# Attention steps with values, denominators and scores of different units side by side, MLP pieces ahead of each attention part, and a second output bank

## The chip, the cores and the metric

The kernel runs on one core of a Trainium2 chip. The metric is device time in microseconds (us). Medians are quoted with the range of the runs. The engines are called PE (TensorE matmul), PEld (its weight loads), ACT (ScalarE), DVE (VectorE), POOL (GpSimd) and SP (SyncE, which issues transfers).

## The reference, cut to what matters

```python
# attention: 8 batches, 8 heads, 576 positions, head size 64
scores = q @ k.T / 8
mask = |i - j| <= 32, or i or j is one of 8 global positions
attn = softmax(where(mask, scores, -1e9))
x = (attn @ v), heads side by side            # 4608 tokens x 512
# MLP
h = x @ w_in                                  # 512 -> 2048
g = h + sin(alpha * h)**2 / (alpha + 1e-9)
out = g @ w_out                               # 2048 -> 512
```

## The kernel before

A batch's attention is 8 units (4 pairs of heads, 2 halves of the sequence). A unit has three stages on PE:

- `stage_Q`: 12 score matmuls into `Sp` (two banks of PSUM, the memory that PE writes its results to), then Exp on ACT into `E` and a multiplication by the mask on DVE.
- `stage_D`: two matmuls with ones into `den` (one bank). ACT takes Ln and Exp of it, which gives the reciprocal `rec`; DVE sums the global columns into `gd`.
- `stage_V`: 12 value matmuls into `num` (one bank). DVE multiplies it by `rec` into `xT`, and sums its global columns into `gn`.

`stage_T` transposes keys and queries of one pair of heads on PE. DVE copies the keys out of the bank `Kps` to `kTw` (0.85 us).

The MLP is done in nine chunks of 512 tokens. `mm1(c)` is the first projection: 16 slots of four matmuls into one of six banks `hb`; then Sin on ACT (`Sb`), a square (`S`) on POOL, DVE or ACT, and an addition on DVE into `H2b`, which frees the bank. `mm2(c)` is the output projection: four token tiles of four pieces of four matmuls. It fills the attention of the next batch, so batch p's attention is mixed with `mm2(p-1)`, and `mm1(p)` follows. The last stage mixes `mm1(8)` with `mm2(7)`, and `mm2(8)` ends the program. The program gives every engine its instructions in the order written. `psA`, `psB` and `psC` in the code are pools of banks.

```python
    def attention(b, psA, t_at):
        ...
        def first(j):
            if j == -2:
                nc.scalar.preload_act_table_set("natural_log_exp_and_others")
            if j + 2 < NUN:
                Es[j + 2] = stage_Q(psA, b, *units[j + 2])
            if 0 <= j + 1 < NUN:
                recs[j + 1] = stage_D(psA, *units[j + 1], Es[j + 1], gd)
            if j + 1 == NUN:
                stage_Gd(gd, gr)
        def second(j):
            if j >= 0:
                stage_V(psA, b, *units[j], Es.pop(j), recs.pop(j), gn)
        parts = []
        for j in range(-2, NUN):
            parts += [partial(first, j), partial(second, j)]
        ...
    # mm2: the tile is copied out by ACT, then stored
                        nc.scalar.copy(out=osb[:], in_=ops[:])
    # which engine squares slot nt of mm1
    sq_late = lambda nt: nc.vector if nt % 5 == 4 else nc.gpsimd
    # batch p > 0: banks of the four tiles, and pieces after each part
                    fill = mm2(p - 1, H2[p - 1], ((psC, "ops"),) * 3 + (((psA, "den") if p > 1 else (psC, "ops")),))
                    counts = [2, 0, 1, 0] + [1, 0] * (NUN)
    # what is left of fill runs after the last part
```

The softmax here doesn't subtract the row's maximum and nothing guards it: scores larger than these inputs give would overflow.

Of the kernel before, what the change touches and what calls it, by code (L numbers as in the profile page):

```python
# [18 lines left out]
def kernel(  # L19
# [11 lines left out]
    nc = tc.nc  # L31
    P = 128
    BF = DT.bfloat16
# [24 lines left out]

    const = ctx.enter_context(tc.tile_pool(name="const", bufs=1))
    qkp = ctx.enter_context(tc.tile_pool(name="qkp", bufs=2))  # L60
    epool = ctx.enter_context(tc.tile_pool(name="epool", bufs=4))
    rpool = ctx.enter_context(tc.tile_pool(name="rpool", bufs=3))
    gpool = ctx.enter_context(tc.tile_pool(name="gpool", bufs=2))

# [266 lines left out]
    def stage_Q(psA, b, hp, hf):  # L331
        Sp = psA.tile([P, 2, CH], F32, name="Sp")
        for u in range(NU):
            i = hf * NU + u
            for t, pr in heads:
                nc.tensor.matmul(  # L336
                    out=Sp[:, t, u * QC : (u + 1) * QC],
                    lhsT=kTw[hp][pr, i, :], rhs=qT[hp][pr, i, :],
                    start=True, stop=True, skip_group_check=True,
                )  # L340
        E = epool.tile([P, 2, EW], BF, name="E")
        nc.scalar.activation(out=E[:], in_=Sp[:, :, 0:EW], func=AF.Exp, scale=scale)  # L342
        mk = MASK[:, hf * NU : (hf + 1) * NU, :].rearrange("p u c -> p (u c)")
        nc.vector.tensor_tensor(  # L344
            out=E[:], in0=E[:], in1=mk[:, None, :].to_broadcast([P, 2, EW]), op=ALU.mult
        )
        return E
# [44 lines left out]
    def stage_Gd(gd, gr):  # L392
        nc.vector.tensor_tensor(out=gr[:], in0=gd[:, 0], in1=gd[:, 1], op=ALU.add)
        nc.vector.reciprocal(out=gr[:], in_=gr[:])
# [11 lines left out]

    units = [(hp, hf) for hp in range(NHP) for hf in range(2)]
    NUN = len(units)

    def attention(b, psA, t_at):  # L410

        Es, recs = {}, {}
        gn = gpool.tile([P, 2, NHP, NG], F32, name="gn")
        gd = gpool.tile([P, 2, NHP, NG], F32, name="gd")
        gr = gpool.tile([P, NHP, NG], F32, name="gr")

        def first(j):
            if j == -2:
                nc.scalar.preload_act_table_set("natural_log_exp_and_others")
            if j + 2 < NUN:  # L420
                Es[j + 2] = stage_Q(psA, b, *units[j + 2])
            if 0 <= j + 1 < NUN:
                recs[j + 1] = stage_D(psA, *units[j + 1], Es[j + 1], gd)
            if j + 1 == NUN:
                stage_Gd(gd, gr)

        def second(j):
            if j >= 0:
                stage_V(psA, b, *units[j], Es.pop(j), recs.pop(j), gn)

        parts = []
        for j in range(-2, NUN):
            parts += [partial(first, j), partial(second, j)]
        for hp, i in t_at.items():
            parts[i] = partial(chain, parts[i], partial(stage_T, b, hp, psA, "qp"))
        return parts, partial(stage_G, b, gn, gr)

    def chain(*fs):
        for f in fs:
            f()  # L440
# [42 lines left out]
    def mm2(c, H2b, pools):  # L483
        slots = []
        st = {}
        G4 = 4
        for ts in range(CH // P):
            for g in range(NT // G4):
                def slot(ts=ts, g=g):
                    if g == 0:  # L490
                        pool, tag = pools[ts]
                        st["o"] = pool.tile([P, DM], F32, name=tag)
                    ops = st["o"]
                    for nt in range(g * G4, (g + 1) * G4):
                        nc.tensor.matmul(  # L495
                            out=ops[:], lhsT=H2b[:, nt, ts * P : (ts + 1) * P],
                            rhs=w_out[:, nt, :],
                            start=(nt == 0), stop=(nt == NT - 1),
                        )
                    if g == NT // G4 - 1:  # L500
                        osb = osbp.tile([P, DM], F32, name="osb")
                        nc.scalar.copy(out=osb[:], in_=ops[:])  # L502
                        r0 = c * CH + ts * P
                        nc.sync.dma_start(out=out[r0 : r0 + P, :], in_=osb[:])
                slots.append(slot)
        return slots
# [12 lines left out]
    def with_extra(parts, extra, start, per):  # L519
        for i in range(start, len(parts)):  # L520
            k_ = (i - start) * per
            if extra[k_ : k_ + per]:
                parts[i] = partial(chain, parts[i], *extra[k_ : k_ + per])
        return extra[(len(parts) - start) * per :] if len(parts) > start else extra
# [19 lines left out]
        for i in range(4)  # L544
    ]

    sq_late = lambda nt: nc.vector if nt % 5 == 4 else nc.gpsimd
    sq_early = lambda nt: nc.vector if nt % 2 else nc.scalar

    ctx.enter_context(tc.manual_schedule())  # L550
    H2 = {}
    NP_ = 2 * (NUN + 2)
    for p in range(NCH):
        fill = []
        late = []
        if p < B:
            with phase_pool("psA", 1) as psA:
                if p == 0:
                    stage_T(0, 0, psA, "qp")
                    globals_all()  # L560
                    for hp in range(NHP):
                        globals_in(0, hp, nc.vector)
                    stage_T(0, 1, psA, "qp")
                    globals_v_all()
                    shift_v(0)
                    global_v(0)
                    parts, last = attention(0, psA, {2: 7, 3: 11})
                    with_extra(parts, w_loads, 6, 1)
                    parts[6] = partial(chain, parts[6], pool_regs)
                    late = load_slots(1, True)  # L570
                    counts = [0] * NP_
                else:
                    fill = mm2(p - 1, H2[p - 1], ((psC, "ops"),) * 3 + (((psA, "den") if p > 1 else (psC, "ops")),))
                    parts, last = attention(p, psA, {2: 4, 3: 8})
                    counts = [2, 0, 1, 0] + [1, 0] * (NUN)
                    if p == 1:
                        shift_v(1)
                        global_v(1)
                        for hp in range(NHP):
                            globals_in(1, hp, nc.vector)  # L580
                        pre = [fill.pop(0) for _ in range(6)]
                        chain(*pre[:4])
                        stage_T(1, 0, psA, "qp")
                        chain(*pre[4:])
                        stage_T(1, 1, psA, "qp")
                    if p + 1 < B:
                        ld = load_slots(p + 1, p == 1)
                        if p == 1:
                            late = ld[5:]
                            ld = ld[:5]  # L590
                            with_extra(parts, ld, 12, 1)
                        else:
                            with_extra(parts, ld, 0, 2)
                        for hp in range(NHP):
                            i_ = (10, 12, 14, 16)[hp]
                            parts[i_] = partial(chain, parts[i_], partial(globals_in, p + 1, hp))
                run(parts + [last], counts + [0], fill)
        else:
            fill = mm2(p - 1, H2[p - 1], ((psC, "ops"),) * 4)
        if p == 0:  # L600
            setup.release()
            hpool = ctx.enter_context(tc.tile_pool(name="hpool", bufs=2))
            spool = ctx.enter_context(tc.tile_pool(name="spool", bufs=4))
            osbp = ctx.enter_context(tc.tile_pool(name="osbp", bufs=2))
        with phase_pool("psB", 6) as psB:
            H2[p] = hpool.tile([P, NT, CH], BF, name="H2b")
            m1 = mm1(p, H2[p], psB, sq_early if p < 2 else sq_late)
            if late:
                with_extra(m1, late, 0, 2)
            if 1 <= p and p + 1 < B:  # L610
                i_ = (10, 13)
                m1[i_[0]] = partial(chain, m1[i_[0]], partial(shift_v, p + 1), partial(global_v, p + 1), partial(stage_T, p + 1, 0, psB, "hb"))
                m1[i_[1]] = partial(chain, m1[i_[1]], partial(stage_T, p + 1, 1, psB, "hb"))
            run(m1, [1] * NT if p == B else [0] * NT, fill if p == B else [])
            if p == NCH - 1:
                for s in mm2(p, H2[p], ((psC, "ops"), (psB, "hb")) * 2):
                    s()
# [30 lines left out]
```

## Time and profile before

| | before |
|---|---|
| median of 4 runs (range) | 404.38 us (401.99 to 405.27) |
| profiled execution, span | 400.5 us |
| PE / ACT / POOL / DVE busy | 85 / 64 / 63 / 59% |
| one period in the middle (batch and its first projection) | 40.4 us |
| of it: PE idle before the first scores | 1.84 us |

The first lines of the page give span and busy time of each engine (share of the span, number of instructions).

```profile
span 400.5 us, 8548 instructions
...
PE 341.6 (85%) x3157; PEld 169.6 (42%) x3208; DVE 236.1 (59%) x549; ACT 256.4 (64%) x437; POOL 250.9 (63%) x394
```

A busy share of 85% does not say where PE is held, so the timeline is read next. Its columns are start and length in us, engine, source line, operation, output and inputs, and in brackets the idle time of the engine before it and what ended that. This is a steady attention step on PE, without transposes:

```profile
203.34 0.37 PE L375 MATMUL num<-E,VW 128*64 128x56 bf16 x12
203.65 0.33 PE L336 MATMUL Sp<-qT,kTw 64*128 64x56 bf16 x12
203.91 0.33 PE L352 MATMUL den<-E,ones 128*64 128x336 bf16 x2
204.17 1.04 PE L495 MATMUL ops<-w_out,H2b 128*128 128x512 bf16 x4
205.14 0.38 PE L375 MATMUL num<-E,VW 128*64 128x56 bf16 x12
```

Starts are to be compared, as ends of matmuls are modelled: 0.31, 0.26, 0.26 and 0.97 us, in all 1.80 us. The shape `128*64` or `64*128` is the part of the array that an instruction uses; it changes four times a step.

At the end of a first-projection stage PE does nothing while DVE makes additions, because the first scores are to be written into banks that these additions free:

```profile
230.25 1.89 PE L458 MATMUL hb<-xT,w_in 128*128 128x512 bf16 x8
233.98 0.33 PE L336 MATMUL Sp<-qT,kTw 64*128 64x56 bf16 x12 [1.84 <-DVE H2b L448]
234.24 1.68 PE L495 MATMUL ops<-w_out,H2b 128*128 128x512 bf16 x7
...
232.53 2.71 DVE L448 SCALAR_TENSOR_TENSOR H2b<-S,recipT,hb 128x512 bf16<-128x512 bf16 x4
```

Over the program the view of waits has for PE (total us, times, longest):

```profile
PE Sp L336 <- DVE H2b L448: 11.5, 6, 2.3
...
PE hb L458 <- POOL xT L402: 6.6, 2, 3.3
```

The second line is the end of batches 0 and 1, where no piece is left to cover POOL's copies of the global tokens. In batch 1 the first matmuls after that wait of 3.31 us run at half clock (the granted clock is 0.50 from 90.7 to 97.5 us), so 43 matmuls take 12.30 us:

```profile
92.15 12.30 PE L458 MATMUL hb<-xT,w_in 128*128 128x512 bf16 x43 [3.31 <-POOL xT L402]
```

The shorter idle (five times 1.84 to 1.85 us, once 2.28) is followed by half clock too, in one of its six occurrences in this execution: 0.50 from 275.0 to 278.5 us. The windows view (stretch, its length, busy time of PE, PEld, DVE, ACT, POOL, granted clock, DMA share, GB/s) around 274 us shows it:

```profile
272.00:274.00 2.00, 0.45 (x3) 0.09 (x1) 2.00 (x4) 1.81 (x3) 0.98 (x2) 1.00 0.00 0
274.00:276.00 2.00, 1.71 (x17) 0.83 (x17) 1.97 (x4) 1.26 (x2) 2.00 (x4) 0.76 0.05 3
276.00:278.00 2.00, 2.00 (x17) 0.61 (x14) 0.00 (x0) 0.00 (x0) 2.00 (x3) 0.50 1.54 98
```

In the last stage ACT copies the last tile of chunk 7, and the next tile, in the same bank, waits 0.67 us for it:

```profile
382.26 0.59 ACT L502 COPY osb<-ops 128x512 f32<-128x512 f32 x1
...
382.89 3.61 PE L495 MATMUL ops<-w_out,H2b 128*128 128x512 bf16 x16 [0.67 <-ACT osb L502]
```

### The profile page before, as it was taken

Reading aid. Unit: us, or ns where it says so; the run is one execution under the profiler, and the core shown is the slowest. Engines: PE = TensorE matmul, PEld = TensorE weight load, DVE = VectorE, ACT = ScalarE, POOL = GpSimd, SP = SyncE. Lnnn points to the kernel's source line nnn. Section 1 sums busy time; section 2 is a strip of 40 time slices with the busy share of each in tenths; the row PEclk is TensorE's granted clock in tenths of the full one; section 3 lists DMA queues with packets and bytes.
Section 4 is the critical chain, followed back from the end, with each engine's and each line's share of the span. In section 5 each row is a group of like instructions: output and inputs, shape, how many; then the busy total and the mean of one; then the engine's idle time right before and its main releaser. Section 6 shows DMA issues by size and latency. Waiting matters only on the chain.

```text
span 400.5 us, 8548 instructions
## 1 busy us (share of the span) xinstructions
PE 341.6 (85%) x3157; PEld 169.6 (42%) x3208; DVE 236.1 (59%) x549; ACT 256.4 (64%) x437; POOL 250.9 (63%) x394
## 2 busy tenths in 40 slices
PE   1137599877979997999899989998999899989996
PEld 0126244443435443444454445443544354434442
DVE  7826388571976297619762877286736873673330
ACT  1057495884988578748784878486838783855421
POOL 8934493329794398929892988398928401874410
PEclk9999999996999999999999999998999999999999
DMA  6999999349999319931993289627924001001012
GB/s 54 146 144 178 202 148 139 46 73 73 160 119 115 107 21 68 172 95 35 59 165 100 46 54 147 114 55 50 153 68 97 1 28 55 26 2 49 32 52 79
DMA packets 133723, 35.31 MB, mean 88 GB/s; under 512 B 123314, under 2 KB 128178, under 8 KB 133682
## 3 DMA queue, kind: packets, MB, share of 16 engines
q0 software_dynamic: 122560, 19.02, 66.4%
q1 hardware_dynamic: 8034, 15.54, 13.4%
q10 hardware_dynamic: 3088, 0.21, 0.8%
q8 instruction: 25, 0.41, 0.4%
q14 instruction: 16, 0.13, 0.1%
HBM read 38.42 MB, written 9.44 MB: 119 GB/s over the span
## 4 chain that ended last, share of the span: by engine, by line
PE 50%; POOL 14%; ACT 12%; issue 11%; DVE 11%; POOLq 1%; ACTq 0%
PE ops L495 23%; PE hb L458 8%; ACT Sb L465 7%; DVE H2b L448 7%; POOL S L473 7%; PE den L495 5%; PE num L375 4%; PE Sp L336 3%; PE den L352 3%; DVE kTw L310 2%; ACT S L471 2%; PE hb L495 2%; POOL KS L95 2%; POOL QS L95 1%; POOL VW L107 1%
## 5 line engine op out<-in xcount | busy, mean ns | idle before, releaser
L458 PE MATMUL hb<-xT,w_in 128*128 128x512 bf16 x559 | 134.9, 387 | 10.1 <-POOL xT L402 6.6
L448 DVE SCALAR_TENSOR_TENSOR H2b<-S,recipT,hb 128x512 bf16<-128x512 bf16 x144 | 101.2, 742 | 53.5 <-POOL S L473 53.5
L473 POOL TENSOR_TENSOR S<-Sb 128x512 bf16<-128x512 bf16 x91 | 94.2, 1063 | 43.5 <-ACT Sb L465 38.6
L465 ACT ACTIVATE Sb<-hb,alphaT 128x512 bf16<-128x512 f32 x144 | 95.1, 686 | 40.6 <-PE hb L458 36.1
L495 PE MATMUL ops<-w_out,H2b 128*128 128x512 bf16 x414 | 109.3, 383 | 4.1 <-issue 1.3
L458 PEld LDWEIGHTS <-w_in 128*128 128x128 bf16 x576 | 56.8, 99 | 79.8 <-issue 19.0
L495 PEld LDWEIGHTS <-H2b 128*128 128x128 bf16 x576 | 51.4, 98 | 60.3 <-issue 8.9
L342 ACT ACTIVATE E<-Sp 128x672 bf16<-128x672 f32 x64 | 46.8, 732 | 19.9 <-PE Sp L336 19.2
L344 DVE TENSOR_TENSOR E<-E,MASK 128x672 bf16<-128x672 bf16 x64 | 33.2, 521 | 41.5 <-ACT E L342 41.5
L402 POOL COPY xT<-xg 128x4 bf16 x64 | 13.0, 203 | 57.5 <-DVE xg L400 54.1
L107 POOL DMA_DIRECT2D VW<-in_v_dram x56 | 42.6, 783 | 1.7 <-DMA KS<-in_k_dram 1.4
L336 PE MATMUL Sp<-qT,kTw 64*128 64x56 bf16 x768 | 22.2, 191 | 16.7 <-DVE H2b L448 11.5
L382 DVE TENSOR_TENSOR xT<-num,rec 128x288 bf16<-128x288 f32 x64 | 29.1, 455 | 11.1 <-PE num L375 7.5
L473 DVE TENSOR_TENSOR S<-Sb 128x512 bf16<-128x512 bf16 x37 | 17.5, 474 | 26.4 <-ACT Sb L465 25.7
L502 ACT COPY osb<-ops 128x512 f32<-128x512 f32 x28 | 16.3, 583 | 25.9 <-PE ops L495 25.3
L375 PEld LDWEIGHTS <-VW 128*64 128x64 bf16 x768 | 18.5, 116 | 27.9 <-issue 14.7
L358 ACT ACTIVATE lnd<-den 128x288 f32<-128x288 f32 x64 | 26.1, 408 | 6.2 <-PE den L352 6.2
L360 ACT ACTIVATE rec<-lnd 128x288 f32<-128x288 f32 x64 | 28.4, 443 | 2.0
L310 DVE COPY kTw<-Kps 128x1344 bf16<-128x1344 bf16 x32 | 27.2, 850 | 3.0 <-PE Kps L304 3.0
L375 PE MATMUL num<-E,VW 128*64 128x56 bf16 x768 | 25.3, 201 | 2.5 <-DVE gn L386 1.4
L336 PEld LDWEIGHTS <-kTw 64*128 64x128 bf16 x768 | 15.8, 96 | 27.4 <-issue 23.7
L352 PE MATMUL den<-E,ones 128*64 128x336 bf16 x128 | 22.7, 347 | 5.1 <-DVE E L344 3.3
(70 smaller groups left out, 305.0 us busy)
## 6 DMA issues: line engine op xcount, KB each, us to landing
out_dram<-osb SPq DMA_DIRECT2D x36, 256.0 KB
VW<-in_v_dram POOLq DMA_DIRECT2D x40, 112.0 KB, 4.4
VW<-VW SPq DMA_DIRECT2D x8, 384.0 KB
KS<-in_k_dram POOLq DMA_DIRECT2D x30, 96.0 KB, 3.7
QS<-in_q_dram POOLq DMA_DIRECT2D x30, 96.0 KB, 3.8
w_in<-in_moe_w_in_dram POOLq DMA_DIRECT2D x4, 512.0 KB, 9.2
w_out<-in_moe_w_out_dram POOLq DMA_DIRECT2D x4, 512.0 KB, 15.5
VW<-VW SPq DMA_DIRECT2D x8, 240.0 KB
```

The lines of the kernel that those rows point to most:

```text
L107: nc.gpsimd.dma_start(out=W[p0 : p0 + n, par, u, :].rearrange("p (h d) -> p h d", d=D), in_=v[b, :, key0 : key0 + n, :].rearrange("h p d - ...
L310: nc.vector.tensor_copy(out=kTw[hp][:, :, 0:KB], in_=bass.AP(tensor=base.tensor, offset=base.offset, ap=[list(base.ap[0]), [QB, NW], [1, KB]],
L336: nc.tensor.matmul(out=Sp[:, t, u * QC : (u + 1) * QC], lhsT=kTw[hp][pr, i, :], rhs=qT[hp][pr, i, :], start=True, stop=True, skip_group_ch ...
L342: nc.scalar.activation(out=E[:], in_=Sp[:, :, 0:EW], func=AF.Exp, scale=scale)
L344: nc.vector.tensor_tensor(out=E[:], in0=E[:], in1=mk[:, None, :].to_broadcast([P, 2, EW]), op=ALU.mult)
L352: nc.tensor.matmul(out=den[pr].rearrange("p u c -> p (u c)"), lhsT=ones[:], rhs=E[:, t, :], start=True, stop=True, skip_group_check=True,)
L375: nc.tensor.matmul(out=num[pr, u, :], lhsT=W[:, i % 2, i // 2, c0 : c0 + 64], rhs=E[:, t, u * QC : (u + 1) * QC], start=True, stop=True, s ...
L448: nc.vector.scalar_tensor_tensor(out=H2b[:, n_, :], in0=s_[:], scalar=recipT[:, n_ : n_ + 1], in1=h_, op0=ALU.mult, op1=ALU.add,)
L458: nc.tensor.matmul(out=h2[:], lhsT=w_in[:, ci, nt * P : (nt + 1) * P], rhs=xT[:, ci, c * CH : (c + 1) * CH], start=(ci == 0), stop=(ci == ...
L465: nc.scalar.activation(out=Sb[:], in_=h2[:], func=AF.Sin, scale=alphaT[:, nt : nt + 1])
L473: eng.tensor_tensor(out=S2[:], in0=Sb[:], in1=Sb[:], op=ALU.mult)
L495: nc.tensor.matmul(out=ops[:], lhsT=H2b[:, nt, ts * P : (ts + 1) * P], rhs=w_out[:, nt, :], start=(nt == 0), stop=(nt == NT - 1),)
```

## The change

Its intent: fewer changes of tiling in a step, more distance between a unit's stages, PE never without work when stages change, and less for ACT and POOL at the ends of the first projection.

```diff
-        def first(j):  ... Q(j+2), D(j+1)
-        def second(j): ... V(j)
+        def step(j):
+            if j == -3:
+                nc.scalar.preload_act_table_set("natural_log_exp_and_others")
+            if j >= 0:
+                stage_V(psA, b, *units[j], Es.pop(j), recs.pop(j), gn)
+            if 0 <= j + 1 < NUN:
+                recs[j + 1] = stage_D(psA, *units[j + 1], Es[j + 1], gd)
+                if j + 2 == NUN:
+                    stage_Gd(gd, gr)
+                    nc.scalar.preload_act_table_set("trig_and_small")
+            if j + 3 < NUN:
+                Es[j + 3] = stage_Q(psA, b, *units[j + 3])
...
-                        nc.scalar.copy(out=osb[:], in_=ops[:])
+                        if ts == CH // P - 1:
+                            nc.vector.tensor_copy(out=osb[:], in_=ops[:])
+                        else:
+                            nc.scalar.copy(out=osb[:], in_=ops[:])
...
-    sq_late = lambda nt: nc.vector if nt % 5 == 4 else nc.gpsimd
+    sq_late = lambda nt: {5: nc.scalar, 10: nc.vector, 15: nc.vector}.get(nt, nc.gpsimd)
...
+                    # placeholders fix the order of the banks num, den, qp, o2, then Sp
-                    fill = mm2(p - 1, H2[p - 1], ((psC, "ops"),) * 3 + (... "den" or "ops",))
-                    counts = [2, 0, 1, 0] + [1, 0] * (NUN)
+                    fill = mm2(p - 1, H2[p - 1], ((psC, "ops"), (psA, "o2")) * 2)
+                    counts = [1] * NP_
+                    counts[-1] = 0
...
-                        pre = [fill.pop(0) for _ in range(6)]     # batch 1
+                        pre = [fill.pop(0) for _ in range(4)]
...
+                    else:                                          # batches 2 to 7
+                        fill.pop(0)()
+                        fill.pop(0)()
```

Cut: a fifth buffer for `E`, and new places for transposes, loads and the copies of the next batch's globals.

More of the change, by code (lines that the diff above doesn't have):

```diff
@@ L60 @@
     qkp = ctx.enter_context(tc.tile_pool(name="qkp", bufs=2))
-    epool = ctx.enter_context(tc.tile_pool(name="epool", bufs=4))
+    epool = ctx.enter_context(tc.tile_pool(name="epool", bufs=5))
     rpool = ctx.enter_context(tc.tile_pool(name="rpool", bufs=3))
@@ L408 @@
     NUN = len(units)
+    LEAD = 3
     def attention(b, psA, t_at):
@@ L415, in attention @@
         gr = gpool.tile([P, NHP, NG], F32, name="gr")
-        def first(j):
-            if j == -2:
+        def step(j):
+            if j == -3:
                 nc.scalar.preload_act_table_set("natural_log_exp_and_others")
-            if j + 2 < NUN:
-                Es[j + 2] = stage_Q(psA, b, *units[j + 2])
+            if j >= 0:
+                stage_V(psA, b, *units[j], Es.pop(j), recs.pop(j), gn)
             if 0 <= j + 1 < NUN:
                 recs[j + 1] = stage_D(psA, *units[j + 1], Es[j + 1], gd)
-            if j + 1 == NUN:
-                stage_Gd(gd, gr)
-        def second(j):
-            if j >= 0:
-                stage_V(psA, b, *units[j], Es.pop(j), recs.pop(j), gn)
-        parts = []
-        for j in range(-2, NUN):
-            parts += [partial(first, j), partial(second, j)]
-        for hp, i in t_at.items():
-            parts[i] = partial(chain, parts[i], partial(stage_T, b, hp, psA, "qp"))
+                if j + 2 == NUN:
[3 more added lines that the diff above has]
+                Es[j + 3] = stage_Q(psA, b, *units[j + 3])
+        parts = [partial(step, j) for j in range(-LEAD, NUN)]
+        for hp, j in t_at.items():
+            parts[j + LEAD] = partial(chain, parts[j + LEAD], partial(stage_T, b, hp, psA, "qp"))
         return parts, partial(stage_G, b, gn, gr)
@@ L551 @@
     H2 = {}
-    NP_ = 2 * (NUN + 2)
+    NP_ = NUN + LEAD
     for p in range(NCH):
@@ L566 @@
                     global_v(0)
-                    parts, last = attention(0, psA, {2: 7, 3: 11})
-                    with_extra(parts, w_loads, 6, 1)
-                    parts[6] = partial(chain, parts[6], pool_regs)
+                    parts, last = attention(0, psA, {2: 0, 3: 2})
+                    with_extra(parts, w_loads, 3, 2)
+                    parts[3] = partial(chain, parts[3], pool_regs)
                     late = load_slots(1, True)
@@ L572 @@
                 else:
-                    fill = mm2(p - 1, H2[p - 1], ((psC, "ops"),) * 3 + (((psA, "den") if p > 1 else (psC, "ops")),))
-                    parts, last = attention(p, psA, {2: 4, 3: 8})
-                    counts = [2, 0, 1, 0] + [1, 0] * (NUN)
+                    for tag, shape, dt_ in (
+                        ("num", [P, NU, QC], F32), ("den", [P, NU, QC], F32),
+                        ("qp", [P, S], BF), ("o2", [P, DM], F32),
+                    ):
+                        psA.tile(shape, dt_, name=tag)
+                    fill = mm2(p - 1, H2[p - 1], ((psC, "ops"), (psA, "o2")) * 2)
+                    parts, last = attention(p, psA, {2: -1, 3: 1})
+                    counts = [1] * NP_
+                    counts[-1] = 0
                     if p == 1:
@@ L580 @@
                             globals_in(1, hp, nc.vector)
-                        pre = [fill.pop(0) for _ in range(6)]
-                        chain(*pre[:4])
+                        pre = [fill.pop(0) for _ in range(4)]
+                        chain(*pre[:2])
                         stage_T(1, 0, psA, "qp")
-                        chain(*pre[4:])
+                        chain(*pre[2:])
                         stage_T(1, 1, psA, "qp")
+                    else:
+                        fill.pop(0)()
+                        fill.pop(0)()
                     if p + 1 < B:
@@ L590 @@
                             ld = ld[:5]
-                            with_extra(parts, ld, 12, 1)
+                            with_extra(parts, ld, 6, 1)
                         else:
-                            with_extra(parts, ld, 0, 2)
+                            with_extra(parts, ld, 0, 4)
                         for hp in range(NHP):
-                            i_ = (10, 12, 14, 16)[hp]
+                            i_ = hp + LEAD + 3
                             parts[i_] = partial(chain, parts[i_], partial(globals_in, p + 1, hp))
```

## The prediction

> **What bounds it now.** TensorE (PE) is 85% busy, ScalarE (ACT) 64%, POOL 63%, VectorE (DVE) 59% (page). In the timeline the middle of the program (batches 2 to 7) repeats every 40.4 us: an attention stage of about 22.9 us with 64 output-projection matmuls ("MLP pieces" of four) between the attention units, then a first-projection stage of about 17.6 us.
> - Attention stage: the windows show PE busy 22.0 of 22.5 us. A steady step takes 1.80 us on PE: values 0.31, scores 0.26, denominators 0.26, MLP piece 0.97. Four 512-column matmuls at 0.216 need 0.86, so about 0.1 us is lost at that change of array tiling; the two denominators (336 columns, side by side: 0.14 estimated from 0.216 per 512) take 0.26. [...] A step has four changes (values 128x64, scores 64x128, denominators 128x64, MLP 128x128).
> - First-projection stage: Sin starts 2.4 us after the first matmul, behind a 1.28 us table load; POOL's squares (1.04 us each) then run back to back, and PE loses about 0.7 us inside. At its end PE idles 1.84 us: the first scores wait for H2b additions that free their PSUM banks (waits: 11.5 us over 6).
> - Batch 1 has no MLP piece left to cover the global-token copies: PE idles 3.3 us, and the next matmuls run at half clock (0.43 us each).
>
> **What the change does.**
> 1. Two MLP pieces (1.73 us) go before the first scores of batches 2 to 7, into the 1.84 us idle. In the built program the first scores now wait for the addition of slot 12, not 13. Gain about 1.8 x 6 = 11 us, on the critical path.
> 2. Values, denominators, scores, piece: values and denominators share a tiling, three changes a step. About 0.1 us x 8 x 7 = 5.5 us.
> 3. Trig table load moved into the attention stage, after the last reciprocal; the last square from POOL (1.04) to DVE (0.41); one square to ACT; the last output copy (0.59) to DVE. Sin starts 1.2 us earlier, but PE can gain only its stalls: about 0.5 x 7 = 3.5 us.
> 4. Batch 1: only 4 pieces ahead, so two remain for its tail: idle 3.3 becomes about 1.6, the half clock shorter or gone; about 3.5 us, as ACT (16 Sin at 0.69, 8 squares at 0.63) then bounds that stage.
> 5. Lead of three, fifth E buffer, second output bank: little alone; batch 0 perhaps 1 us. The last stage (28.6 us, PE 27.7) gains nothing.
>
> Sum about 24 us. I take off 2: by its durations ACT needs 13.5 us of the 14.3 that eight steps will take, and will sometimes hold scores back.
>
> **Prediction:** 383 us; 8 in 10 between 376 and 392. Faster by over 2%: 0.95; within 2%: 0.04; slower by over 2%: 0.01.
>
> **What would show it.** Period 40.4 -> about 37.3. PE's wait of the first scores for H2b, 11.5 us -> under 2. Steady step 1.80 -> 1.70, with values-to-denominators at about 0.31 and denominators-to-scores near 0.15. First Sin 1.1 us after the stage's first matmul. At batch 1, PE's wait for POOL's copies 3.3 -> 1.6, then no half clock.
>
> **What would make it wrong.** Scores waiting for ACT's Exp in every step (step stays 1.8); denominators saving no time beside values; the fourth piece waiting for the last H2b additions; POOL or DVE still limiting the first-projection stage; low-clock phases.

The sum is 24 us (11 + 5.5 + 3.5 + 3.5 + 1 is 24.5), less 2. The 0.216 us is measured: 16 output-projection matmuls take 3.46 us from start to the next start (212.97 to 216.43 in the profile of the kernel before). That the 0.1 us belongs to the change of tiling was the estimate from 0.97 less 0.86; e3 and e10 test it.

## The result

| | before | after |
|---|---|---|
| median of 4 runs (range) | 404.38 (401.99 to 405.27) | 386.49 (386.09 to 386.79) |
| ratio after / before, 95% interval | | 0.9566 (0.9520 to 0.9611) |
| profiled execution, span | 400.5 | 385.0 |

The change gains 17.9 us by the medians; 383 was predicted, with 376 to 392 as the range.

```profile
span 385.0 us, 8609 instructions
...
PE 336.2 (87%) x3208; PEld 162.9 (42%) x3208; DVE 244.9 (64%) x551; ACT 258.4 (67%) x435; POOL 249.3 (65%) x394
```

Source lines of the MLP are one or two lower in the new file (first projection L458 is L457, output projection L495 is L494), and the trace prints the new bank `o2` as `o`. A steady step now reads:

```profile
193.40 0.38 PE L375 MATMUL num<-E,VW 128*64 128x56 bf16 x12
193.61 0.31 PE L352 MATMUL den<-E,ones 128*64 128x336 bf16 x2
193.85 0.33 PE L336 MATMUL Sp<-qT,kTw 64*128 64x56 bf16 x12
194.12 1.04 PE L494 MATMUL o<-w_out,H2b 128*128 128x512 bf16 x4
195.11 0.37 PE L375 MATMUL num<-E,VW 128*64 128x56 bf16 x12
```

The starts are 0.21, 0.24, 0.27 and 0.99 us apart, 1.71 us in all (the next step takes 1.68). The values take 0.21 us, where they took 0.31 when scores followed them.

At the stage's end two pieces (eight matmuls) run first, and the scores find their banks free (the view of waits has no line any more of scores that wait for H2b):

```profile
181.17 1.89 PE L457 MATMUL hb<-xT,w_in 128*128 128x512 bf16 x8
182.89 1.89 PE L494 MATMUL ops<-w_out,H2b 128*128 128x512 bf16 x8
184.72 0.33 PE L336 MATMUL Sp<-qT,kTw 64*128 64x56 bf16 x12
```

At batch 1 the wait is 1.46 us where it was 3.31, and the matmuls after it run at full clock (44 in 9.67 us):

```profile
90.68 9.67 PE L457 MATMUL hb<-xT,w_in 128*128 128x512 bf16 x44 [1.46 <-POOL xT L402]
```

Three things in the new trace were not forecast. First, in the last stage PE waits 3.01 us for DVE's copy of chunk 7's last tile, and the next 16 matmuls take 4.95 us, not 3.61 (clock 0.50 from 365.2 to 368.6 us):

```profile
363.18 2.06 DVE L447 SCALAR_TENSOR_TENSOR H2b<-S,recipT,hb 128x512 bf16<-128x512 bf16 x3
365.15 0.68 DVE L502 COPY osb<-ops 128x512 f32<-128x512 f32 x1
...
365.89 4.95 PE L494 MATMUL ops<-w_out,H2b 128*128 128x512 bf16 x16 [3.01 <-DVE osb L502]
```

Second, in the first-projection stage the square of slot 10 takes DVE 1.28 us (with no square on POOL it takes 0.41 to 0.43). POOL's run of four squares, started at 174.72, ends at 178.75, 0.28 us before DVE's one ends at 179.03. The copy of the keys is late by that, and the next transposes wait for it:

```profile
174.72 4.03 POOL L472 TENSOR_TENSOR S<-Sb 128x512 bf16<-128x512 bf16 x4 [0.53 <-ACT Sb L464]
...
177.76 1.28 DVE L472 TENSOR_TENSOR S<-Sb 128x512 bf16<-128x512 bf16 x1 [0.22 <-ACT Sb L464]
...
179.62 0.84 DVE L310 COPY kTw<-Kps 128x1344 bf16<-128x1344 bf16 x1
...
180.51 0.42 PE L304 MATMUL Kps<-identb,KS 96*128 96x96 bf16 x6 [0.47 <-DVE kTw L310]
```

Third, in the attention stage the mask multiplication of the last unit takes 1.01 us, where the median is 0.51, while POOL copies the next batch's globals; values that wait for DVE's sums behind it lose 0.32 us:

```profile
198.86 0.27 POOL L292 COPY kTw<-GT 128x96 bf16<-128x96 bf16 x1
...
198.89 1.01 DVE L344 TENSOR_TENSOR E<-E,MASK 128x672 bf16<-128x672 bf16 x1 [0.41 <-ACT E L342]
...
200.44 0.38 PE L375 MATMUL num<-E,VW 128*64 128x56 bf16 x12 [0.32 <-DVE gn L386]
```

Both DVE instructions that lengthen run beside POOL instructions: the square takes 1.28 us when POOL's square has 0.99 us to go (slot 10 here), 0.58 beside POOL's squares in e5, 0.44 at 0.16 us to go (slot 15, at 183.87), and 0.41 to 0.43 with no square on POOL; the mask multiplication takes 1.01 against 0.51. The H2b addition does not lengthen: it takes 0.73 to 0.75 us in both kernels (144 each), although POOL squares beside it. What makes the one kind longer and not the other was not shown.

To place gains and losses, each profiled span is cut at the first w_in matmul of a chunk, read from the timeline. "Pieces first" and "mended" are the experiments e11 and e12 below.

| stretch, us | before | pieces first (e11) | after | mended (e12) |
|---|---|---|---|---|
| start to chunk 0 | 46.6 | 46.0 | 46.3 | 46.3 |
| chunk 0 to 1 (batch 1) | 45.6 | 46.5 | 44.4 | 43.6 |
| chunk 1 to 2 (batch 2) | 43.2 | 40.6 | 38.1 | 38.1 |
| chunk 2 to 7 (five periods) | 203.5 | 193.4 | 191.2 | 189.4 |
| chunk 7 to end | 61.6 | 61.6 | 65.0 | 60.3 |

So the change gains 0.3, 1.2, 5.1 and 12.3 us, and loses 3.4 us at the end: 15.5 us between these two executions. How well such a stretch repeats is seen in e1, whose program is the same as the changed kernel's until the last stage: its five periods took 190.2 us, not 191.2 (one of 38.4 us became one of 38.0). Differences under 1 us in that row are not resolved; in the row of batch 1 the same two profiles differ by 1.0 us (44.4 and 43.4).

### The profile page after: what moved, and what is told of

Read it like the earlier page. It is cut to its first block, busy times and chain, and to the rows that moved or that the text cites. A ratio compares the mean times of both kernels' runs of the same rounds, so it can differ in the third digit from the quotient of the medians.

```text
span 385.0 us, 8609 instructions
## 1 busy us (share of the span) xinstructions
PE 336.2 (87%) x3208; PEld 162.9 (42%) x3208; DVE 244.9 (64%) x551; ACT 258.4 (67%) x435; POOL 249.3 (65%) x394
## 4 chain that ended last, share of the span: by engine, by line
PE 52%; ACT 18%; DVE 10%; issue 7%; POOL 7%; DMA 3%; POOLq 1%; ACTq 0%; DVEq 0%
PE hb L457 22%; PE ops L494 13%; PE o L494 8%; ACT Sb L464 6%; ACT E L342 4%; DMA KS<-in_k_dram 3%; DVE H2b L447 3%; PE num L375 3%; ACT S L470 2%; DVE S L472 2%; DVE kTw L310 2%; ACT lnd L358 2%; PE hb L494 2%; ACT rec L360 2%; PE Sp L336 2%
## 5 line engine op out<-in xcount | busy, mean ns | idle before, releaser
L457 PE MATMUL hb<-xT,w_in 128*128 128x512 bf16 x576 | 133.1, 384 | 6.0 <-POOL xT L402 4.8
L464 ACT ACTIVATE Sb<-hb,alphaT 128x512 bf16<-128x512 f32 x144 | 96.6, 684 | 55.2 <-PE hb L457 53.9
L447 DVE SCALAR_TENSOR_TENSOR H2b<-S,recipT,hb 128x512 bf16<-128x512 bf16 x144 | 102.6, 741 | 29.3 <-POOL S L472 28.8
L472 POOL TENSOR_TENSOR S<-Sb 128x512 bf16<-128x512 bf16 x91 | 92.6, 1040 | 34.1 <-ACT Sb L464 31.5
L457 PEld LDWEIGHTS <-w_in 128*128 128x128 bf16 x576 | 56.5, 99 | 74.4 <-issue 10.9
L494 PE MATMUL ops<-w_out,H2b 128*128 128x512 bf16 x320 | 81.7, 385 | 3.2 <-DVE osb L502 3.0
L494 PEld LDWEIGHTS <-H2b 128*128 128x128 bf16 x576 | 50.6, 98 | 58.6 <-issue 7.3
L344 DVE TENSOR_TENSOR E<-E,MASK 128x672 bf16<-128x672 bf16 x64 | 34.1, 534 | 32.9 <-ACT E L342 32.2
L494 PE MATMUL o<-w_out,H2b 128*128 128x512 bf16 x224 | 54.7, 380 | 0.0
L342 ACT ACTIVATE E<-Sp 128x672 bf16<-128x672 f32 x64 | 45.9, 717 | 4.1 <-PE Sp L336 4.0
L100 POOL DMA_DIRECT2D QS<-in_q_dram x30 | 23.2, 774 | 3.0 <-DMA QS<-in_q_dram 3.0
L324 ACT COPY qT<-qp 128x576 bf16<-128x576 bf16 x20 | 12.7, 633 | 18.4 <-PE ops L268 13.2
```

The lines of the kernel that those rows point to most:

```text
L342: nc.scalar.activation(out=E[:], in_=Sp[:, :, 0:EW], func=AF.Exp, scale=scale)
L344: nc.vector.tensor_tensor(out=E[:], in0=E[:], in1=mk[:, None, :].to_broadcast([P, 2, EW]), op=ALU.mult)
L447: nc.vector.scalar_tensor_tensor(out=H2b[:, n_, :], in0=s_[:], scalar=recipT[:, n_ : n_ + 1], in1=h_, op0=ALU.mult, op1=ALU.add,)
L457: nc.tensor.matmul(out=h2[:], lhsT=w_in[:, ci, nt * P : (nt + 1) * P], rhs=xT[:, ci, c * CH : (c + 1) * CH], start=(ci == 0), stop=(ci == ...
L464: nc.scalar.activation(out=Sb[:], in_=h2[:], func=AF.Sin, scale=alphaT[:, nt : nt + 1])
L472: eng.tensor_tensor(out=S2[:], in0=Sb[:], in1=Sb[:], op=ALU.mult)
```

## The experiments

Series 1 is e1 to e4, series 2 e5 to e8, series 3 e9 to e12; each ran on one chip with its own runs of the kernel before. All gave correct results. "Changed kernel" is the one after the change, 386.49 us, ratio 0.9566.

| run | what | median us (range) | ratio to before (95%) |
|---|---|---|---|
| e1 | chunk 7's last copy on ACT | 382.48 (380.79 to 382.90) | 0.9469 (0.9432 to 0.9506) |
| e2 | square of slot 10 on ACT | 384.52 (383.38 to 385.47) | 0.9505 (0.9466 to 0.9544) |
| e3 | values, scores, denominators | 385.74 (384.69 to 386.16) | 0.9543 (0.9501 to 0.9584) |
| e4 | no pieces ahead | 396.21 (394.65 to 399.14) | 0.9825 (0.9762 to 0.9888) |
| e5 | no early trig table | 384.40 (383.60 to 386.34) | 0.9518 (0.9459 to 0.9576) |
| e6 | one output bank | 395.93 (394.23 to 397.44) | 0.9823 (0.9759 to 0.9886) |
| e7 | global copies on DVE | 387.47 (387.12 to 387.96) | 0.9598 (0.9539 to 0.9656) |
| e8 | all mended, globals on DVE | 381.92 (381.21 to 383.24) | 0.9472 (0.9411 to 0.9534) |
| e9 | mended, no early trig table | 382.46 (382.01 to 383.21) | 0.9466 (0.9438 to 0.9494) |
| e10 | mended, values, scores, denominators | 382.01 (381.17 to 383.48) | 0.9458 (0.9427 to 0.9488) |
| e11 | kernel before with pieces first only | 390.34 (389.86 to 390.81) | 0.9664 (0.9627 to 0.9701) |
| e12 | mended, globals on POOL | 380.59 (379.59 to 381.55) | 0.9423 (0.9393 to 0.9452) |

### e1: where the last stage lost its time

```diff
-                        if ts == CH // P - 1:
+                        if ts == CH // P - 1 and c < NCH - 2:
```

> The changed kernel with one thing undone: the output copy of the fourth token tile of the last interleaved stage (chunk 7) goes back from VectorE to ScalarE; all other fourth-tile copies stay on VectorE (this also returns the very last copy of chunk 8). Theory A (the last stage lost 3.4 us because that copy stands on VectorE behind the square and three H2b additions of the last slot, and TensorE then sits 3.0 us and restarts at half clock): 386.5 falls to about 383 us, TensorE's wait for the copy before the last 64 matmuls goes from 3.0 to about 0.7 us, and the first 16 of them take about 3.6 us, not 4.95. Rival B (the last stage lost its time elsewhere, for example at its start, where the first slot waits for H2b additions): the time stays within 0.7 us of 386.5.

Measured: 382.48 us, 4.0 less. In the profile of this run ACT copies at once, while DVE is still at its additions, the wait (0.67 us) and the 16 matmuls after it (3.61 us) are as before the change, and the clock is 1.000:

```profile
360.82 0.58 ACT L504 COPY osb<-ops 128x512 f32<-128x512 f32 x1
...
361.46 3.61 PE L494 MATMUL ops<-w_out,H2b 128*128 128x512 bf16 x16 [0.67 <-ACT osb L504]
```

Theory A holds. (The edit also returns the last copy of chunk 8 to ACT.) Moving the copy to DVE frees ACT at the start of the stages in the middle, where DVE is idle (2.43 us before the copy at 167.48 in the changed kernel), but in the last stage the same line of code puts it behind a square and three additions.

### e2: the square that meets POOL

```diff
-    {5: nc.scalar, 10: nc.vector, 15: nc.vector}
+    {5: nc.scalar, 10: nc.scalar, 15: nc.vector}
```

> The changed kernel with the square of slot 10 on ScalarE, not VectorE. Theory A (in the first-projection stage that square takes 1.28 us on VectorE [...], and holds back the copy of the keys, for which the next transposes wait 0.47 us): the wait of the second transposes is gone and the six periods lose about 0.4 us each, 384 us in all. Rival B (the stage is bound by VectorE's additions or by POOL whatever that square does; ScalarE takes 0.63 us more and pushes the Sin behind it): within 0.7 us of 386.5, and the stage stays 15.6 us.

Measured: 384.52 us, 2.0 less, and no run of it reaches the range of the changed kernel; but the two ran in different series, and their ratio intervals overlap. The five periods take 189.5 us, 1.7 less than in the profile of the changed kernel and 0.7 less than in e1. From the start of the first projection to the first piece is 14.8 us where it was 15.6, but the first scores now wait 0.6 us for H2b additions in five batches. Theory A holds in its mechanism (the transposes wait no more) and in sign; the gain is 0.1 to 0.3 us a period, not 0.4, because part of it is given back in that new wait.

### e3: what a change of tiling costs

The order of `stage_D` and `stage_Q` in a step is swapped.

```diff
-            D(j+1), then Q(j+3)
+            Q(j+3), then D(j+1)
```

> The changed kernel with the order of a step values, scores, denominators (as before the change) in place of values, denominators, scores: four changes of array tiling a step, not three. Theory A (each change costs about 0.1 us of TensorE): a step with scores goes from 1.69 to 1.80 us; with five such steps a batch and seven batches about 4 us more, 390.5 us. Rival B (the changes cost nothing by themselves, and steps are held by ScalarE and VectorE): within 0.8 us of 386.5.

Measured: 385.74 us, no slower, which is rival B's figure. But the step itself is longer, just as theory A says:

```profile
193.38 0.38 PE L375 MATMUL num<-E,VW 128*64 128x56 bf16 x12
193.68 0.33 PE L336 MATMUL Sp<-qT,kTw 64*128 64x56 bf16 x12
193.94 0.33 PE L352 MATMUL den<-E,ones 128*64 128x336 bf16 x2
194.21 1.04 PE L494 MATMUL o<-w_out,H2b 128*128 128x512 bf16 x4
195.18 0.38 PE L375 MATMUL num<-E,VW 128*64 128x56 bf16 x12
```

It takes 1.80 us, as before the change, against 1.69 on average of the two steps quoted above. The values take 0.30 us when scores come next and 0.21 us when denominators do; followed by a piece, which changes the tiling too, they take 0.30 (201.77 to 202.07 here) or 0.31 (163.51 to 163.82 in the changed kernel). So about 0.1 us goes with the change of tiling after them. What pays for part of it is waits: in the period shown, PE waits twice for the `gn` or `gd` sums in the changed kernel (0.3 us each) and never with this order (over the program 4.2 against 1.2 us), probably because there the mask multiplication comes earlier in DVE's queue than the sum of the denominators. The five periods take 190.8 us, against 191.2 and 190.2 for the two executions of the changed order, so they do not separate the two.

The medians flatter this order, because the clock favours it. The 3.01 us wait of the last stage is in both profiles, but only in the changed kernel's does half clock follow it:

```profile
364.30:365.90 1.60, 0.01 (x1) 0.01 (x1) 1.53 (x3) 0.00 (x0) 0.00 (x0) 0.78 0.00 0
...
364.30:365.90 1.60, 0.01 (x1) 0.01 (x1) 1.54 (x3) 0.00 (x0) 0.00 (x0) 1.00 0.00 0
```

(The first line is the changed kernel, the second e3; the third number from the end is the clock.) After the wait 16 matmuls took 4.95 us in the changed kernel and 3.61 in e3:

```profile
365.89 3.61 PE L494 MATMUL ops<-w_out,H2b 128*128 128x512 bf16 x16 [3.01 <-DVE osb L502]
```

After the same wait they took 3.61 us in e6, 5.30 in e2 and e5, and 6.50 in e7; why the clock falls after the wait in one profile and not in another was not shown. The last stage took 65.0 us in the changed kernel and 63.6 in e3. Three of the four runs of e3 had the full clock (1.000), those of the changed kernel 0.990 to 0.996. By these means the clock can have cost the changed kernel up to 2 us more (an estimate: half a per cent of 385 us). So e3 does not show that the order is worth nothing; e10 compares the orders without that wait.

### e4: without the pieces ahead

```diff
-                    else:
-                        fill.pop(0)()
-                        fill.pop(0)()
```

> The changed kernel without the two MLP pieces ahead of the first scores in batches 2 to 7 (they run at the batch's end). Theory A (they fill an idle of up to 1.8 us in which the first scores wait for the H2b additions): TensorE waits again at the first scores of each batch, 1.0 to 1.8 us, and the time rises by 6 to 11 us to 392 to 397. Rival B (the new bank order, by which scores wait for an earlier addition, already does most of it): rise of under 4 us.

Measured: 396.21 us, 9.7 more; theory A holds in its total. PE's waits of scores for H2b additions come back with 5.6 us in six batches (at most 1.3 each). That is half of the 11.5 us of the kernel before, so the rest of the change, by rival B its bank order, removes the other half by itself. And PE's waits of scores for ACT's Exp rise from 4.1 to 8.1 us: in batches 2 to 7 the second score stage waits 0.60 to 0.72 us for an Exp. What delays that Exp was not shown.

### e5: without the early table load

```diff
-                    nc.scalar.preload_act_table_set("trig_and_small")
```

> The changed kernel without the early load of the trig table (the 1.28 us load falls again before the first Sin of each first-projection stage). Theory A (the early load is what lets TensorE run the first eleven slots of that stage in 9.50 us where it took 9.94 before): about 0.4 us a stage over seven stages, 389.5 us, with the stretch back at about 9.9 us. Rival B (the stage's length is set by its end, where the second transposes wait for VectorE, so the start does not count): within 0.8 us of 386.5. Rival C (ScalarE is the limit of the attention stage and the load there costs as much as it saves): faster than 386.5.

Measured: 384.40 us (383.60 to 386.34). The first eleven slots take 9.89 us again, as theory A says, but the time does not rise: theory A falls. The median lies where rival C put it, but nothing else supports that rival: the periods do not get shorter. The five periods take 190.1 us, equal to those of e1, so in the changed kernel the early load gains nothing. The trace shows why: without it, slot 10's square falls at another moment of POOL's squares and takes 0.58 us, not 1.28, in all five periods, and the transposes do not wait.

```profile
178.05 0.58 DVE L471 TENSOR_TENSOR S<-Sb 128x512 bf16<-128x512 bf16 x1
...
180.15 0.42 PE L304 MATMUL Kps<-identb,KS 96*128 96x96 bf16 x6
```

The lower median of this run is no proof against the early load: two of its four runs had the full clock (1.000), none of the changed kernel's (0.990 to 0.996). The changed kernel, e5 and e7 all have the 3.01 us wait of e1's theory in their last stage, and how long the clock is low after it differs from execution to execution (the 16 matmuls after it took 4.95, 5.30 and 6.50 us).

### e6: the second bank

```diff
-                    fill = mm2(p - 1, H2[p - 1], ((psC, "ops"), (psA, "o2")) * 2)
+                    fill = mm2(p - 1, H2[p - 1], ((psC, "ops"),) * 4)
```

> The changed kernel with all four output tiles of a chunk in one PSUM bank in the attention batches (the second bank stays allocated, unused). Theory A (the second bank matters at the batch's end alone, where the fourth tile follows the third at once and ScalarE copies the third only after the 1.28 us table load): TensorE waits there 1.3 to 1.8 us in each of six or seven batches, 8 to 11 us more, 394 to 398 us. Rival B (pieces of different tiles are far enough apart; the bank is worth nothing): within 1 us of 386.5.

Measured: 395.93 us, 9.4 more. Theory A holds:

```profile
PE ops L494 <- ACT osb L504: 9.9, 7, 1.6
```

This is the worth of a second bank at the batch's end, not the worth of this part of the change: the kernel before already put its fourth tile into another bank (`den`) in batches 2 to 7.

### e7: the global copies

```diff
-    parts[i_] = partial(chain, parts[i_], partial(globals_in, p + 1, hp))
+    parts[i_] = partial(chain, parts[i_], partial(globals_in, p + 1, hp, nc.vector))
```

> The changed kernel with the copies of the next batch's global keys and queries on VectorE, not on POOL. Theory A (POOL's copies collide with VectorE's mask multiplication of the last unit, 1.01 to 1.07 us where it otherwise takes 0.51, and the values two steps later wait for it): that multiplication is back at 0.5 us, TensorE's waits for the gn sums fall by about 0.4 us a batch, 384 to 385 us. Rival B (eight more copies of about 0.2 us in VectorE's queue cost TensorE as much or more): 386.5 or slower.

Measured: 387.47 us, no faster, as rival B has it. The collision is gone: over the period examined no mask multiplication is longer than 0.51 us, and PE's waits for `gn` fall from 3.1 to 2.1 us over the program. The five periods take 190.2 us, within the spread of the changed kernel. The total is higher because the first 16 matmuls after the wait in the last stage took 6.50 us here, and 4.95 in the changed kernel. Theory A's mechanism is right and its gain is not there; e8 and e12 compare the two places of the copies without that wait, though in different series.

### e8 and e12: a version that takes the losses away

```diff
-                        if ts == CH // P - 1:
+                        if ts == CH // P - 1 and c < NCH - 2:
-    {5: nc.scalar, 10: nc.vector, 15: nc.vector}
+    {5: nc.scalar, 10: nc.scalar, 15: nc.vector}
-                for s in mm2(p, H2[p], ((psC, "ops"), (psB, "hb")) * 2):
+                for s in mm2(p, H2[p], ((psB, "hb"), (psC, "ops")) * 2):
```

e8 has the edit of e7 as well; e12 leaves the global copies on POOL.

> A try at a better version: the copy at the end of chunk 7 on ScalarE, the square of slot 10 on ScalarE, the global copies on VectorE, and the first output tile of the last chunk in a bank of the first projection's pool, so that it waits for no copy. If these losses add up: 386.5 less 4 (measured with the first alone), less 2 (the second alone), less 0 to 2, less 0.7 for the wait for the copy before the last chunk: 378 to 380 us. If mending one uncovers another limit (VectorE's additions, ScalarE), 381 to 382.

> The mended version with the global copies back on POOL (chunk 7's last copy and slot 10's square on ScalarE, first tile of the last chunk in another bank). If the global copies on VectorE bought nothing: 381 to 382, as the version with them. If they cost: about 380. If they helped: 383.

Measured: 381.92 us for e8 and 380.59 us for e12, in different series, with intervals of the ratio that overlap. e8 missed its first forecast (378 to 380) and fell where another limit was expected (381 to 382); e12 lies between "about 380" and "381 to 382". Of the 6.7 us that its parts promised (4.0, 2.0 and 0.7), e12 has 5.9, so the losses mostly add up. The global copies on DVE bring nothing that shows: five periods of 189.6 us with them and 189.4 without. Whether they cost a little is not resolved. e12 is the fastest version, 5.9 us faster than the changed kernel by the medians, and its ratio interval (0.9393 to 0.9452) lies below that of the changed kernel.

### e9: the early table load again, in the mended version

The edit is that of e5, made to e12.

> As the previous one, without the early load of the trig table. Theory A (the early load was useless only because it moved slot 10's square on VectorE into POOL's way; with that square on ScalarE the load is worth its 0.4 us in the stage's first eleven slots): about 2.5 us slower than the previous one. Rival B (what is gained at the stage's start is lost at its end, where the first scores wait for the H2b additions and VectorE or POOL sets the pace): within 1 us of it.

Measured: 382.46 us, 1.9 more than e12 in the same series; no run of either reaches the other's range. The five periods take 191.0 us against 189.4. Theory A holds: with the square of slot 10 out of POOL's way, the early load is worth about 0.3 us a period (1.7 over five), a little under the 0.4 us of the stage's start.

### e10: the order again, in the mended version

The edit is that of e3, made to e12.

> As the mended version with global copies on POOL, with the order values, scores, denominators. Theory A (with this order TensorE pays one more tiling change, about 0.1 us in five steps a batch, but has no waits for VectorE's gn and gd sums, as in the first run of this order, and the two are equal): within 1 us of the mended version. Rival B (with the other losses mended the tiling change shows): 3 to 4 us slower.

Measured: 382.01 us, 1.4 more than e12; the ranges overlap a little (381.17 to 383.48 against 379.59 to 381.55), and so do the ratio intervals. Both had the full clock or nearly (0.998 to 1.000). It is between the two expectations. The five periods take 190.3 against 189.4 us, so the order of the change seems to be worth about 0.2 us a period, two fifths of the 0.5 us that five steps of 0.1 us would give; one pair of profiles does not resolve this 1.0 us surely.

### e11: one part alone, in the kernel before

```diff
                     counts = [2, 0, 1, 0] + [1, 0] * (NUN)
+                    if p > 1:
+                        counts = [1, 0] * (NUN + 2)
...
+                    else:
+                        fill.pop(0)()
+                        fill.pop(0)()
```

> The kernel before the change with one part of it alone: in batches 2 to 7 two MLP pieces ahead of the first scores, then one piece a unit; order, lead of two, banks and all else as before. Theory A (filling the idle in which the first scores wait for H2b additions is by itself the largest part of the gain): TensorE's wait of scores for H2b additions falls from 11.5 us to under 2, and 404 becomes 394 to 396. Rival B (the idle returns as another wait, as the first denominators then wait for Exp and mask, because the lead is two units only): 398 to 402.

Measured: 390.34 us, 14.0 less than before by the medians. Theory A holds, and beyond its range. The waits of scores for H2b fall from 11.5 us to one of 0.55 us, in batch 2; rival B's wait of denominators for the mask is there, but is 0.17 us:

```profile
109.47 1.89 PE L495 MATMUL ops<-w_out,H2b 128*128 128x512 bf16 x8
111.91 0.33 PE L336 MATMUL Sp<-qT,kTw 64*128 64x56 bf16 x12 [0.55 <-DVE H2b L448]
...
113.64 0.33 PE L352 MATMUL den<-E,ones 128*64 128x336 bf16 x2 [0.17 <-DVE E L344]
```

A steady period falls from 40.4 to 38.7 us, 1.7 us as costed, so the six handovers give about 10.4 us. The rest goes together with the clock: the timed runs of the kernel before have a mean granted clock of 0.983 to 0.987, those of e11 0.990 to 0.996. In the profile shown before, one of the six idles of 1.84 to 2.28 us was followed by 3.4 us of half clock, and that period took 41.9 us where its neighbours took 40.3; e11 has no such period. By an estimate from these means (0.01 of 400 us) the clock is worth up to 4 us, which is enough for the 3.6 us left; that a few more such events in the median run account for the rest was not shown separately.

## Why the prediction was right, point by point

1. **Pieces ahead of the scores.** Predicted: about 1.8 us in each of six batches, 11 us. Measured: e11, this part alone, 14.0 us, of which 1.7 us a period (10.4 us in six) is the idle itself. Taking it out of the changed kernel (e4) costs 9.7 us. Mechanism and size of a handover are right; the low clock after such an idle (once in six in the profile before) was not costed.
2. **Three tilings a step, not four.** Predicted: 0.1 us x 8 x 7 = 5.5 us. The step did fall from 1.80 to 1.69 us, but the order is worth about 1.4 us in the mended version (e10); e3 can't resolve it. Two terms were mis-sized: five of the eight units a batch have a full step, and PE then waits for DVE's sums (4.2 us over the program against 1.2 with the other order). The prediction also put the saving in the wrong place: it forecast 0.31 us from values to denominators and 0.15 us from denominators to scores, and they are 0.21 and 0.24. The saving stands in the distance from the values to what follows them: 0.30 to 0.31 us before another tiling, 0.21 before the same one.
3. **Table load, squares, last copy.** Predicted: 0.5 us x 7 = 3.5 us. Sin does start 1.1 us after the stage's first matmul (168.41 after 167.28), and eleven slots take 9.50 us where they took 9.94. But the stage stayed at 15.6 us, because slot 10's square met POOL's and the key copy came late. With that mended, the early load is worth 1.9 us (e9).
4. **Batch 1.** Predicted: 3.5 us, with a wait of about 1.6 us and no half clock. Measured: a wait of 1.46 us and full clock; against e11, which leaves batch 1 as before, the stretches of batches 1 and 2 are 2.1 and 2.4 us shorter, 4.5 us together. Right in mechanism and about in size: part of it is the shorter steps of both batches, and the first of these stretches is uncertain by 1 us. No experiment changed the pieces of batch 1 alone.
5. **Lead, fifth buffer, banks; batch 0.** Predicted: 1 us. Measured: 0.3 us to the first projection of chunk 0, which is within the spread (45.6 to 46.9 us in the profiles of the experiments). What the lead of three, the fifth buffer, the new places of the transposes, and the second bank beyond the `den` bank of before are worth was not tested by itself.
6. **The last stage.** Predicted: "gains nothing". It lost 3.4 us, and e1 gave back 4.0. This step failed in its mechanism, where 2 and 3 failed in size: the prediction names the last copy on DVE only as a relief of ACT, which it is where DVE is idle, and did not follow the same line of code into the last stage.

The period fell to 38.2 us (191.2 / 5), not to the forecast 37.3. Of 22 us predicted, 17.9 came: the two handovers gave more than stated, the tiling and the squares less, and the last stage took 3 to 4 back. That the total came so close is partly luck: terms 2 and 3, 9 us of the 24, gave little (e3, e5, e10), and about 4 us more than forecast came from the handovers, in good part, by the estimate under e11, a gain in clock that was not costed. ACT, for which 2 us were taken off, was not what PE waited for in a steady step; where it waited, it was for DVE's sums.

## What to carry to other kernels

Look at the places where one stage hands over to the next before looking at steady steps: one rearrangement of two pieces of independent work gave 14.0 us alone here, where the whole change gave 17.9, and the better step order about 1.4. (The parts do not simply add: taken out of the whole, the same rearrangement is worth 9.7 us.) When one line of code moves work to another engine, follow it into every stage that uses it, the last above all, and ask what stands before it in that engine's queue. Here a step shorter by 0.11 us on the busiest engine was worth about 1.4 us in all (e10), with PE waiting 4.2 us for DVE's sums in the changed kernel against 1.2 in e3. And before two medians a microsecond apart are compared, look at the granted clock of their runs.
